# Light convolution and maxout on one core: tokens loaded with the rows ahead of them, weights split in twelve units, and a new opening order

## The chip, the cores and the metric

One core of a Trainium2 chip runs the whole program. Its engines are named as the profile names them: PE (TensorE, with PEld for its weight loads), DVE (VectorE), ACT (ScalarE), POOL (GpSimd) and SP (SyncE, which here issues nearly all DMAs and passes signals between matmuls). The metric is the device time of one execution in microseconds (us), lower is better; given is the median of several runs.

## The reference

`x` is 8 x 4160 tokens of 192 numbers, `weight_gen` has 8 heads x 7 taps for each token. The first half is a causal light convolution with softmaxed taps, the second a maxout layer. Cut to what matters:

```python
w = weight_gen - np.max(weight_gen, axis=-1, keepdims=True)
w = np.exp(w)
w = w / (np.sum(w, axis=-1, keepdims=True) + 1e-09)
x_pad = np.concatenate([np.zeros((B, 6, D), np.float32), x], axis=1)
idx = np.arange(S)[:, None] + np.arange(7)[None, :]
x_unf = x_pad[:, idx, :].reshape(B, S, 7, H, group)
x = np.einsum('bshk,bskhg->bshg', w, x_unf).reshape(B * S, D)
h = np.maximum(np.maximum(x @ w1, x @ w2), x @ w3)
return (h @ w_out).astype(np.float32)
```

`w1`, `w2`, `w3` (192 x 768) and `w_out` (768 x 192) arrive as 64-bit floats: each value is two 32-bit words, the high one with sign, exponent and the first mantissa bits.

## The kernel before, in words

**Tiling.** The 33,280 tokens lie on 128 partitions, 260 consecutive tokens each; 16 partitions hold one batch. Work goes in 65 chunks of 4 tokens per partition (512 tokens). Loads go in groups of chunks ("supers"): chunk 0 alone, then three chunks each. A group's tile `xt` holds its tokens and the 6 ahead of them, `wt` its taps.

**Attention half of a chunk.** `softmax(s)` (L210) works on a whole group: a maximum on DVE (`red`), a subtraction on POOL, Exp on ACT, sum, addition and reciprocal on DVE (`den`), a product on POOL. `product(c, t)` (L234, "x") multiplies the taps of one token on POOL into `r`; `total(c, t)` (L257, "+") sums `r` over the taps on DVE into `acc`. `transpose(c)` ("t") brings `acc` to features on partitions, for chunks 0 to 2 with PE into two banks of PSUM, later with DVE and ACT. `parts(c)` (L293, "p") makes a high and a low part of it (`xa_hi`, `xa_lo`, `xb`, `xc`), which for chunks 0 to 2 costs ACT four copies and DVE two subtractions.

**Maxout half.** `up` (L341) makes 18 outputs of 128 features x 512 tokens in PSUM (`ph`, 8 buffers that everything in PSUM shares), each from 9 matmuls on half the rows of the array; two chains of half-row matmuls run side by side. Of the three outputs of one block, ACT copies the first to `m` (L376) and DVE takes the maximum with the second and the third (L378), so a chunk has 12 such maxima. Then ACT and POOL make `h_hi` and `h_lo` (L381, L385), and `down` (L389) multiplies them by `w_out`; the products of chunk c - 1 stand after the twelfth output of chunk c.

**Weights.** Before the matmuls of chunk 0 can go on, each weight must be split into a high and a low fp32r part. `split` (L453) does it for 18 units: `a0` to `a8` (rows 0 to 127 of w1 to w3, 256 columns each), `b0` to `b2` (rows 128 to 191, 384 columns), `d0` to `d5` (`w_out`, 192 columns). Each unit costs ACT an Abs (L470), a copy of half-words (L476), the high part (L493) and a conversion (L497), DVE five operations (L481, L483, L488, L494, L495) and POOL a product (L498); a `b` unit also needs four copies on ACT to both halves of the partitions (L553).

**The order.** All instructions are pinned in the order in which the program writes them. Time is counted in ticks, 22 to a chunk; `OPENING` names for the first ticks what is written at each (one step of a unit, product, sum and so on), with -1 for all that stands ahead of the first matmul. After the opening fixed ticks place everything. Each engine takes its own instructions strictly in this order.

**Loads.** `load_super` (L183) fills `xt` of a group. Where the group begins within the first 6 tokens of a partition, the rows ahead lie at the end of the partition before: DVE sets them to zero (L196), one DMA of 128 partitions brings the tokens (L197), and 8 DMAs, one for each batch and 15 partitions each, bring the rows ahead (L202). For group 0, half of these 8 stand on ACT's queue. The raw words of the weights go into buffers that are used later for other things (`h_hi`, `h_lo`, `raw_a`, `room`).

Of the kernel before, what the change touches and what calls it, by code (L numbers as in the profile page):

```python
# [21 lines left out]
P = 128  # L22

OPENING = {
    -1: (
# [1 line left out]
        "a1 b0 s0 b1 +0.2 s1 a3 a3 a6"  # L30
# [79 lines left out]

# [20 lines left out]

# [573 lines left out]
```

## Time and profile before

| | |
|---|---|
| median of 3 runs | 1697.91 us (1697.88 to 1699.43) |
| the profiled execution, its own time | 1699.39 us |
| its span, first to last instruction | 1697.6 us |
| PE busy in the span | 1657.2 us (98%) |
| DVE, ACT, POOL busy | 1124.6, 1145.8, 1426.2 us |
| first matmul of chunk 0 | 29.96 us |
| first matmul of `down` for chunk 0 | 81.86 us |

The profile gives one execution. A row of its groups says how often an instruction ran, its mean in ns and how long the engine stood idle before it; a row of its timeline begins with the start and the duration in us; a row by windows gives busy us and the number of instructions of each engine in a stretch. Matmuls are pipelined, so two hundred of them in 20 us and a hundred in 20 us can both look busy: in the opening the count is what to read.

### The profile page before, as it was taken

The numbers are of one execution on the slowest core, as the hardware profiler recorded it, in microseconds if no ns is written. First come the engines' busy times: TensorE is split into PE (matmuls) and PEld (weight loads), VectorE is DVE, ScalarE is ACT, GpSimd is POOL, SyncE is SP. The second block draws the span as 40 slices with busy tenths as digits, with TensorE's granted clock in tenths as the row PEclk, the third lists the DMA queues.
The fourth block names the chain that finished last, engine by engine and source line by source line (L and its number), as shares of the span: only waits on it lengthen the run. The fifth ranks groups of instructions, "written<-read, shape, count | busy, mean of one in ns | idle before, by whom it ended". The sixth has DMA issues, their size and how long they took to land.

```text
span 1697.6 us, 42191 instructions
## 1 busy us (share of the span) xinstructions
PE 1657.2 (98%) x16794; PEld 1466.1 (86%) x16794; DVE 1124.6 (66%) x1552; ACT 1145.8 (67%) x2896; POOL 1426.2 (84%) x844
## 2 busy tenths in 40 slices
PE   3899999999999999999999999999999999999999
PEld 2598889889889889889988988988988988988998
DVE  7966766666666666666666666666666666666653
ACT  5657667667666766766766766766776776676672
POOL 6888888989888888888888888988888888888872
PEclk9999999999999999999999999999999999999999
DMA  7010101101010110101010110101011010101000
GB/s 236 1 70 10 70 29 52 70 20 60 20 70 15 66 70 21 60 21 70 11 70 21 60 70 20 61 20 70 11 70 61 27 63 20 70 11 46 20 11 29
DMA packets 20422, 79.51 MB, mean 47 GB/s; under 512 B 2320, under 2 KB 5128, under 8 KB 17536
## 3 DMA queue, kind: packets, MB, share of 16 engines
q1 hardware_dynamic: 20104, 76.54, 11.9%
q8 instruction: 131, 2.15, 0.5%
q14 instruction: 67, 0.55, 0.1%
q10 hardware_dynamic: 120, 0.28, 0.0%
HBM read 51.25 MB, written 25.56 MB: 45 GB/s over the span
## 4 chain that ended last, share of the span: by engine, by line
PE 94%; DVE 3%; ACT 1%; DMA 1%; POOL 1%; SPq 0%; issue 0%; DVEq 0%
PE ph L329 94%; DVE acc L261 1%; DVE m L378 0%; DMA wt<-in_weight_gen_dram 0%; DVE ph L483 0%; POOL r L246 0%; DVE ph L488 0%; DVE e L495 0%; DVE ph L481 0%; DVE ph L494 0%; DMA xt<-in_x_dram 0%; SPq L529 0%; ACT room L290 0%; SPq L521 0%; POOL h_lo L385 0%
## 5 line engine op out<-in xcount | busy, mean ns | idle before, releaser
L246 POOL TENSOR_TENSOR r<-xt,wt 128x1344 f32<-128x1344 f32 x260 | 721.4, 2814 | 0.6 <-DMA xt<-in_x_dram 0.4
L378 DVE TENSOR_TENSOR m<-ph,m 128x512 f32<-128x512 f32 x780 | 520.6, 685 | 197.4 <-PE ph L329 113.7
L329 PE MATMUL ph<-xa_hi,wa_hi 64*128 64x512 f32 x2340 | 630.8, 391 | 9.4 <-DVE m L378 3.1
L385 POOL TENSOR_TENSOR h_lo<-m,h_hi 128x512 fp32r<-128x512 f32 x390 | 503.3, 1301 | 161.7 <-ACT h_hi L381 157.0
L329 PE MATMUL ph<-xa_lo,wa_hi 64*128 64x512 f32 x2340 | 626.9, 388 | 1.0 <-DVE xa_lo L304 1.0
L329 PE MATMUL ph<-xa_hi,wa_lo 64*128 64x512 f32 x2340 | 626.1, 387 | 1.1 <-POOL wa_lo L498 1.1
L329 PE MATMUL ph<-xb,wb_hi 64*128 64x512 f32 x2340 | 626.0, 387 | 0.0
L329 PE MATMUL ph<-wo,h_hi 64*128 64x384 f32 x3120 | 595.5, 355 | 0.0
L329 PE MATMUL ph<-wo,h_lo 64*128 64x192 f32 x3120 | 522.3, 247 | 0.0
L381 ACT CAST h_hi<-m 128x512 fp32r<-128x512 f32 x390 | 241.8, 621 | 409.7 <-DVE m L378 406.6
L261 DVE TENSOR_REDUCE acc<-r 128x192 f32<-128x1344 f32 x260 | 401.8, 1547 | 125.5 <-POOL r L246 125.5
L290 ACT COPY room<-room 32x128 f32<-32x128 f32 x1488 | 440.8, 296 | 25.7 <-DVE room L284 7.5
L329 PE MATMUL ph<-xc,wb_lo 64*128 64x512 f32 x1170 | 453.1, 387 | 0.1
L329 PEld LDWEIGHTS ph<-wo,h_lo 64*128 64x128 f32 x3120 | 398.8, 188 | 2.5
L329 PEld LDWEIGHTS ph<-wo,h_hi 64*128 64x128 f32 x3120 | 398.4, 184 | 2.9 <-issue 0.4
L329 PEld LDWEIGHTS ph<-xa_hi,wa_hi 64*128 64x128 f32 x2340 | 338.7, 185 | 53.9 <-DVE m L378 3.9
L329 PEld LDWEIGHTS ph<-xa_hi,wa_lo 64*128 64x128 f32 x2340 | 338.4, 185 | 42.0 <-POOL wa_lo L498 1.5
L329 PEld LDWEIGHTS ph<-xa_lo,wa_hi 64*128 64x128 f32 x2340 | 338.7, 185 | 38.7 <-DVE xa_lo L304 1.5
L329 PEld LDWEIGHTS ph<-xb,wb_hi 64*128 64x128 f32 x2340 | 338.7, 185 | 38.4 <-ACT xb L308 0.3
L376 ACT COPY m<-ph 128x512 f32<-128x512 f32 x390 | 221.8, 586 | 38.5 <-PE ph L329 35.3
L411 DVE TENSOR_TENSOR o<-ph,ob 128x192 f32<-128x192 f32 x260 | 86.7, 353 | 234.5 <-ACT ob L410 234.5
L329 PEld LDWEIGHTS ph<-xc,wb_lo 64*128 64x128 f32 x1170 | 216.3, 185 | 20.9 <-POOL wb_lo L498 0.5
(54 smaller groups left out, 702.6 us busy)
## 6 DMA issues: line engine op xcount, KB each, us to landing
xt<-in_x_dram SPq DMA_DIRECT2D x20, 1728.0 KB, 7.1
out_dram<-o SPq DMA_DIRECT2D x64, 384.0 KB, 2.3
wt<-in_weight_gen_dram SPq DMA_DIRECT2D x21, 336.0 KB, 3.0
h_hi<-in_moe_w_dram SPq DMA_DIRECT2D x6, 256.0 KB, 4.8
xt<-in_x_dram SPq DMA_DIRECT2D x1, 1536.0 KB, 9.3
h_lo<-in_moe_w_dram SPq DMA_DIRECT2D x6, 192.0 KB, 4.8
room<-in_moe_w_out_dram SPq DMA_DIRECT2D x1, 1152.0 KB, 8.1
xt<-in_x_dram SPq DMA_DIRECT2D x1, 960.0 KB, 5.2
```

Of the source, the lines that this page charges most:

```text
L246: nc.gpsimd.tensor_tensor(r.rearrange("p (h g) k -> p k h g", g=G), xt[:, la + t : la + t + K].rearrange("p k (h g) -> p k h g", g=G), wt[ ...
L261: nc.vector.tensor_reduce(state["acc", c][:, t], r, axis=AX.X, op=ALU.add)
L290: pin(nc.scalar.copy(to[:, :, p : p + 32], blocks[p : p + 32, :, f : f + 32]))
L329: ins = nc.tensor.matmul(ph[:, :n], w[h], v[h], start=begins and half == 0 and q == 0, stop=ends and half == 1 and q == len(terms) - 1,)
L376: pin(nc.scalar.copy(m[:, :N], ph[:, :N]))
L378: pin(nc.vector.tensor_tensor(m[:, :N], ph[:, :N], m[:, :N], op=ALU.max))
L381: later(1, lambda: pin(nc.scalar.copy(hi, m[:, :N])))
L385: nc.gpsimd.tensor_tensor(lo, m[:, :N], hi.bitcast(F32), op=ALU.subtract)
L411: pin(nc.vector.tensor_tensor(o[:, t], po[:, :D], ob, op=ALU.add))
```

## The change

**Loads of groups 0 and 1.** A partition's tokens and the 6 (or 2) rows ahead of them are contiguous in memory, so each partition now loads both with one run: one DMA for partitions 16 to 127 (112), one for 1 to 15, one for partition 0, all on SP. What comes from the batch before is then cleared: for group 0 by `clear` ("c0"), two operations on DVE that mask with `inside` (0 on the first partition of a batch); for group 1 by a DMA of zeros taken from `ident`. `inside` comes from an iota on POOL and two small operations on DVE. ACT's table for Exp is loaded by an early activation on one column.

**Groups.** Chunk 1 is a group of its own, so chunks 2 to 4 are the next. The sum of the softmax of the first three groups lies in PSUM.

**Split.** 12 units: `a0` to `a5` (256 or 512 columns), `b0` to `b2` and `d0` to `d2` (384 each). In the six units of `WHOLE`, Abs takes its scale 2^-112 and DVE clamps once (`min`); in the other six the clamp is two Relu on ACT. Then follow on DVE two `scalar_tensor_tensor`, on ACT the high part (`d2` on DVE) and the low part as a difference, on POOL for `a4`, `b0`, `b2`, `d0` and on DVE for the others. The high part of a `b` unit is used from where it lies for one half; the other half comes by two DMAs (`b0`, `b1`) or two copies on ACT (`b2`) instead of four.

**Order.** The loads stand as `s0 a0 b s1 a1 a2 d` (before: `s0 a0 b a1 s1 a2 d`), and `OPENING` is new. The diff, cut to its core:

```diff
 OPENING = {
     -1: (
-        "x0.0 x0.1 a0 a0 a1 a0 a1 x0.3 a2 a0 x0.2 a2 +0.0 a2 b0 b0 s1 +0.1 a1 a2 b0 +0.3 s1 "
+        "x0.3 a0 x0.0 a0 a1 a0 a0 a0 b2 a1 +0.3 a1 a0 a1 x0.2 t0 s1 b2 x0.1 a1 a1 b2 b1 b1 "
...
+LO_ON_POOL = ("a4", "b0", "b2", "d0")
+BY_DMA = ("b0", "b1")
+HI_ON_VECTOR = ("d2",)
+WHOLE = ("a0", "a1", "a2", "a4", "b1", "b2")
+FIRST = 2
+LOADS = "s0 a0 b s1 a1 a2 d"
+UNITS_A = ((0, 0, 1), (0, 1, 3), (1, 0, 2), (1, 2, 3), (2, 0, 2), (2, 2, 3))
+UNITS_D = ((0, 2), (2, 4), (4, 6))
...
-        if len(supers) == 1 or len(supers[-1]) == SC:
+        if len(supers) <= FIRST or len(supers[-1]) == SC:
...
-            pin(nc.vector.memset(xt[:, :z], 0.0))
-            pin(nc.sync.dma_start(out=xt[:, z : n + PAD], in_=xf[:, : a + n]))
-            for b in range(B):
-                queue = nc.scalar if s == 0 and b % 2 else nc.sync
...
+            for p, q in ((PB, P), (1, PB)):
+                pin(nc.sync.dma_start(out=xt[p:q, : n + PAD], in_=rows[p - 1 : q - 1]))
+            pin(nc.sync.dma_start(out=xt[:1, z : n + PAD], in_=xf[:1, : a + n]))
+            if s == 0:
+                pin(nc.vector.memset(xt[:1, :z], 0.0))
...
+    def clear(s):
+        n = PAD // 2
+        for t in (n, 0):
+            xs = state["x", s][:, t : t + n].rearrange("p t d -> p (t d)").bitcast(I32)
+            pin(nc.vector.tensor_tensor(
+                    xs, xs, inside.broadcast_to([P, n * D]), op=ALU.bitwise_and))
+            yield
+    def clear_by_dma(s, n):
...
+        pin(nc.sync.dma_start(out=xt, in_=zeros))
...
+    def split(flat, hi, lo, name, into, **sizes):
...
+            scale = 2.0**-112 if whole else 1.0
+            pin(nc.scalar.activation(u, high.bitcast(F32), AF.Abs, scale=scale))
+        if whole:
+            pin(nc.scalar.activation(low, halfwords[..., 1], AF.Copy, scale=7.49 / 65536))
+        else:
...
+            pin(eng(to, halfwords[..., 1:3]))
+        yield
...
+        if whole:
+            pin(eng.tensor_scalar(u, u, W_MAX, None, op0=ALU.min))
+            parts = (u.bitcast(U32), 3, low, ALU.logical_shift_left)
+        else:
...
+                pin(nc.scalar.activation(u, upper, AF.Relu, bias=over, scale=-1.0))
+                yield
+                upper, bias, scale = u, span, -float(1 << 19)
+            pin(nc.scalar.activation(v.bitcast(U32), upper, AF.Relu, bias=bias, scale=scale))
+            parts = (low, 13, v.bitcast(U32), ALU.logical_shift_right)
+        yield
+        pin(nc.vector.scalar_tensor_tensor(
+                v.bitcast(U32), *parts[:3], op0=parts[3], op1=ALU.bitwise_or))
+        yield
+        w = prep.tile([P, NU], F32, name="w", bufs=3)[:, :n] if name in LO_ON_POOL else v
+        pin(nc.vector.scalar_tensor_tensor(
...
+        w = w.rearrange(into, **sizes)
+        if name in HI_ON_VECTOR:
+            pin(nc.vector.tensor_copy(hi, w))
+        else:
+            pin(nc.scalar.copy(hi, w))
+        yield
+        eng = nc.gpsimd if name in LO_ON_POOL else nc.vector
+        pin(eng.tensor_tensor(lo, w, hi.bitcast(F32), op=ALU.subtract))
```

What this moves shows in three places. On DVE, the opening up to the first sum of a token; this was the order before (L481 to L495 are the split of `a0` and `a1`, `f` and `e` its intermediate values, L261 the sum of products `r`):

```order
L481 TENSOR_SCALAR ph<-ph 128x256
L483 TENSOR_SCALAR ph<-ph 128x256
L488 SCALAR_TENSOR_TENSOR ph<-h_hi,ph 128x256
L494 TENSOR_SCALAR ph<-f 128x256
L495 TENSOR_SCALAR e<-ph 128x256
```

And this is the order now (L182 clears the rows ahead in `xt`, L468, L484, L491 and L508 are a split, L246 is the sum):

```order
L182 TENSOR_TENSOR xt<-xt,edges 128x576 x2
L468 TENSOR_SCALAR ph<-ph 128x256
L484 SCALAR_TENSOR_TENSOR ph<-ph,low 128x256
L491 SCALAR_TENSOR_TENSOR ph<-h_hi,ph 128x256
L468 TENSOR_SCALAR ph<-ph 128x512
L246 TENSOR_REDUCE acc<-r 128x192
L484 SCALAR_TENSOR_TENSOR ph<-ph,low 128x512
L508 TENSOR_TENSOR wa_lo<-ph,wa_hi 128x2x128
```

The five operations of a unit on DVE became two to four, three in most units, and for eight of the twelve units one of them is the low part, which stood on POOL.

On DVE again, around the 14th to 16th maximum of the program (L378, `m_718` and `m_702`; chunk 0 has twelve, so these are of chunk 1), before. The other rows are splits of `w_out`, each `ph` number a unit, `f` and `e` their intermediate values:

```order
L378 TENSOR_TENSOR m_718<-ph_705,m_718 128x512
L481 TENSOR_SCALAR ph_751<-ph_751 128x192
L483 TENSOR_SCALAR ph_751<-ph_751 128x192
L488 SCALAR_TENSOR_TENSOR ph_751<-room_88,ph_751 128x192
L378 TENSOR_TENSOR m_702<-ph_716,m_702 128x512
L481 TENSOR_SCALAR ph_755<-ph_755 128x192
L483 TENSOR_SCALAR ph_755<-ph_755 128x192
L488 SCALAR_TENSOR_TENSOR ph_755<-room_88,ph_755 128x192
L378 TENSOR_TENSOR m_718<-ph_739,m_718 128x512
L494 TENSOR_SCALAR ph_751<-f_753 128x192
L495 TENSOR_SCALAR e_752<-ph_751 128x192
```

The same place now, from the last split to the 16th maximum (L359 is the maximum, `m_630` and `m_646` those of the 13th to 16th; L484 to L508 is the end of the split of `d2`, L288 and L293 the parts of chunk 2, L246 a sum of chunk 3):

```order
L484 SCALAR_TENSOR_TENSOR ph_303<-low_304,ph_303 128x384
L491 SCALAR_TENSOR_TENSOR ph_303<-room_89,ph_303 128x384
L503 CAST wo_84<-ph_303 128x2x192
L508 TENSOR_TENSOR wo_84<-ph_303,wo_84 128x2x192
L288 TENSOR_TENSOR xa_lo_667<-ph_656,xa_hi_666 128x512
L293 TENSOR_TENSOR xb_668<-ph_657,xc_669 64x512
L359 TENSOR_TENSOR m_630<-ph_614,m_630 128x512
L359 TENSOR_TENSOR m_646<-ph_633,m_646 128x512
L246 TENSOR_REDUCE acc_706<-r_704 128x192
L359 TENSOR_TENSOR m_630<-ph_644,m_630 128x512
L359 TENSOR_TENSOR m_646<-ph_684,m_646 128x512
```

All splits now stand ahead of the 13th maximum, and the parts of chunk 2 with them; before, nine operations of splits stood behind the 16th.

On SP, the queue of loads before (L189 are taps, L197 tokens, L202 the rows ahead, L521 and L529 weights):

```order
L189 DMA wt<-in_weight_gen_dram 128x224
L197 DMA xt<-in_x_dram 128x768
L202 DMA xt<-in_x_dram 15x1152 x4
L521 DMA h_hi<-in_moe_w_dram 128x512 x3
L529 DMA h_lo<-in_moe_w_dram 64x3x256 x6
L521 DMA h_hi<-in_moe_w_dram 128x512 x3
L189 DMA wt<-in_weight_gen_dram 128x672
L197 DMA xt<-in_x_dram 128x3072
L202 DMA xt<-in_x_dram 15x384 x8
```

And now (L160 are taps, L170 and L171 tokens with the rows ahead, L532 and L540 weights):

```order
L160 DMA wt<-in_weight_gen_dram 128x224
L170 DMA xt<-in_x_dram 112x1920
L170 DMA xt<-in_x_dram 15x1920
L171 DMA xt<-in_x_dram 1x768
L532 DMA h_hi<-in_moe_w_dram 128x512 x3
L540 DMA h_lo<-in_moe_w_dram 64x3x256 x6
L160 DMA wt<-in_weight_gen_dram 128x224
L170 DMA xt<-in_x_dram 112x1920
L170 DMA xt<-in_x_dram 15x1920
L171 DMA xt<-in_x_dram 1x1536
L532 DMA h_hi<-in_moe_w_dram 128x512 x3
L532 DMA raw_a<-in_moe_w_dram 128x512 x3
```

Six DMAs of SP and four of ACT ahead of the first weights became four of SP. Behind the rows shown stand `w_out`, the zeros for group 1, the taps and tokens of group 2 (chunks 2 to 4), and only then the four DMAs that bring the other halves of `b0` and `b1`.

More of the change, by code (lines that the diff above doesn't have):

```diff
@@ L169, in lightconv_maxout_kernel @@
     wo = const.tile([P, NJ, 2 * D], F32R, name="wo")
-    F_MAX = float(np.array(0x47EFFFFF, np.uint32).view(np.float32))
-    F_MIN = float(np.array(0x38000000, np.uint32).view(np.float32))
-    NU = 3 * P
+    E_MIN = (1023 - 127) << 4
+    E_MAX = (255 << 4) - 1
+    NU = 4 * P
+    edges = const.tile([P, P], F32, name="edges")
+    over, span, below, warm = (edges[:, k : k + 1] for k in range(4))
+    inside = edges[:, 4:5].bitcast(I32)
+    F_MAX = float(np.array((E_MIN + E_MAX) << 16 | 0xFFFF, np.uint32).view(np.float32))
+    W_MAX = float(np.array(255 << 20, np.uint32).view(np.float32) * (1 - 2.0**-24))
     halves = (slice(0, DB), slice(DB, P))
@@ L259, in total @@
         r = state.pop(("r", c, t))
+        if ("acc", c) not in state:
+            state["acc", c] = att.tile([P, TC, D], F32, name="acc")
         pin(
@@ L348, in up @@
             j = 2 * jp + odd
-            terms = [(wa_hi[:, j, i], xa_hi), (wa_hi[:, j, i], xa_lo), (wb_hi[:, j, i], xb)]
+            terms = [(wa_hi[:, j, i], xa_hi), (wa_hi[:, j, i], xa_lo)]
+            terms.append((wb_hi[:, j if half == 0 else j ^ 1, i], xb))
             if half == odd:
@@ L540, in prepare_a @@
     def prepare_a(u):
-        jp, i = divmod(u, 3)
-        raw = raws_a[jp][:, i].rearrange("p (j n) w -> p j n w", j=2)
-        pair = slice(2 * jp, 2 * jp + 2)
-        yield from split(raw, wa_hi[:, pair, i], wa_lo[:, pair, i])
-    def prepare_b(jp):
-        raw = raw_b[:, jp]
-        hi = prep.tile([P, 3, P], F32R, name="hi", bufs=1)
-        yield from split(raw, hi, wb_lo[:, jp])
-        for odd, h in enumerate(halves):
-            for to in halves:
-                pin(nc.scalar.copy(wb_hi[to, 2 * jp + odd], hi[h].bitcast(F32)))
@@ new lines, in prepare_b @@
+    def prepare_b(jp):
+        flat = raw_b[:, jp].rearrange("p i n w -> p (i n) w")
+        hi, other = (wb_hi[:, 2 * jp + odd] for odd in range(2))
+        yield from split(flat, hi, wb_lo[:, jp], f"b{jp}", "p (i n) -> p i n", n=P)
+        yield
+        for h, to in zip(halves, reversed(halves)):
+            if f"b{jp}" in BY_DMA:
+                pin(nc.sync.dma_start(out=other[to].bitcast(F32), in_=hi[h].bitcast(F32)))
+            else:
+                pin(nc.scalar.copy(other[to], hi[h].bitcast(F32)))
@@ L566, in lightconv_maxout_kernel @@
+    nc.gpsimd.memset(span, float(E_MAX << 19))
+    nc.gpsimd.memset(below, float(-(E_MIN << 19)))
+    pin(nc.scalar.activation(warm, below, AF.Exp))
+    state["now"] = -1
+    for name in LOADS.split():
+        if name[0] == "s":
+            load_super(int(name[1:]))
+        elif name[0] == "a":
+            load_up(int(name[1:]))
+        else:
+            {"b": load_rest, "d": load_down}[name]()
     make_identity(nc, ident)
+    clear_by_dma(1, PAD - TC)
     NC = len(chunks)
@@ L585, in stage @@
             finish(f"s{super_of[c]}")
+            if c == 0 and t[0] == PAD // 2:
+                if "c0" not in running:
+                    stage("c0")
+            elif c == 0:
+                finish("c0")
         elif name[0] == "+":
```

182 lines of the change are left out of this document (74 added, 108 removed), and 23 rows, old and new, of the table OPENING.

## The prediction, as put on record

> **What bounds the kernel now.** First the windows of the trace, core 0: busy us and number of instructions of PE, PEld, DVE, ACT and POOL, then the granted clock, the DMA share and GB/s.
>
> ```profile
> 30.00:40.00 10.00, 8.84 (x41) 6.28 (x43) 9.55 (x20) 7.38 (x17) 8.57 (x5) 1.00 0.62 243
> 50.00:60.00 10.00, 7.39 (x54) 4.46 (x52) 9.65 (x20) 8.07 (x18) 4.22 (x5) 1.00 0.00 1
> 70.00:80.00 10.00, 8.03 (x58) 5.68 (x56) 9.35 (x23) 5.93 (x17) 10.00 (x9) 0.88 0.00 0
> 80.00:90.00 10.00, 10.00 (x111) 8.73 (x109) 5.91 (x9) 3.94 (x8) 8.24 (x6) 0.95 0.01 2
> 400.00:800.00 400.00, 400.00 (x4106) 356.33 (x4103) 264.15 (x354) 277.82 (x708) 347.74 (x202) 1.00 0.13 49
> ```
>
> In the steady part PE runs 10.26 matmuls per us. Between 30 and 80 us it runs 41 to 58 in 10 us, though it counts as busy there, and DVE is at 93 to 97%. From 80 us on PE is at full rate and DVE at 59%. So the kernel has an opening that DVE bounds and a long part that PE bounds. Next the waits of PE from 100 to 1600 us (us in total, times, longest), then the end of the chain of waits, and from PE's timeline the first matmul of `down`:
>
> ```profile
> PE ph L329 <- DVE o L411: 0.2, 1, 0.2
> ```
> ```profile
> 170.18 1523.98 PE ph L329 x14710
> ```
> ```profile
> 81.86 0.44 PE L329 MATMUL ph<-wo,h_hi 64*128 64x384 f32 x1
> ```
>
> PE waits 0.2 us in 1500, and the chain stays on PE to the end. So the time is that of the first `down` plus a constant, as long as the other engines keep ahead of PE behind it: what the first `down` gains, the kernel gains. I cost the change as the move of 81.86, in three stretches.
>
> **The start of DVE's splits.** The timeline of SP's queue, ACT, DVE and POOL (start, duration, what ended the idle time):
>
> ```profile
> 2.09 3.59 SPq L202 DMA_DIRECT2D xt<-in_x_dram  x4
> ...
> 6.08 1.51 SPq L521 DMA_DIRECT2D h_hi<-in_moe_w_dram  x3
> ```
> ```profile
> 4.02 1.28 ACT L222 ACT_TABLE_LOAD   x1 [4.02 <-DVE red L215]
> ...
> 8.70 0.40 ACT L470 ACTIVATE ph<-h_hi 128x256 f32<-128x256 f32 x1 [3.00 <-DMA h_hi<-in_moe_w_dram]
> ```
> ```profile
> 9.14 0.43 DVE L481 TENSOR_SCALAR ph<-ph 128x256 f32<-128x256 f32 x1 [2.42 <-ACT ph L470]
> ```
> ```profile
> 7.84 7.65 POOL L246 TENSOR_TENSOR r<-xt,wt 128x1344 f32<-128x1344 f32 x3 [0.40 <-DMA xt<-in_x_dram]
> ```
>
> The first weights left SP at 6.08, behind four issues of rows ahead, 3.59 us together. Now four single issues stand there; at 0.4 to 0.9 us each the weights leave at about 3, and would land at 5.7 by the same 2.6 us of flight. Against that, the tokens are two and a half times the bytes, and DVE has two clears (128x576) ahead of the first split, which wait for the tokens. I take them at 0.7 us each, by the nearest row (128x512, 0.68, below), and the tokens at 6.5 us. POOL's first product shows them complete at 7.84 before. Then DVE starts to split at 8.3, with 7.2 (tokens 1.1 us earlier than that) and 10.5 (2.2 later) as bounds. Gain 0.8, from -1.4 to 1.9. The table load, 1.28 us on ACT behind the first `red`, now stands at the start, where ACT waits anyway; it hides behind the DMAs and is worth nothing, unless the tokens come first.
>
> **DVE from there to the 16th maximum.** The groups of DVE up to 90 us (count, busy us, mean ns, idle before), and the 16th maximum in its timeline:
>
> ```profile
> L261 DVE TENSOR_REDUCE acc<-r 128x192 f32<-128x1344 f32 x12 | 18.3, 1543 | 0.0
> L378 DVE TENSOR_TENSOR m<-ph,m 128x512 f32<-128x512 f32 x20 | 13.3, 683 | 1.7 <-PE ph L329 1.6
> ...
> L488 DVE SCALAR_TENSOR_TENSOR ph<-h_hi,ph 128x256 uint32<-128x256 uint32 x6 | 2.6, 429 | 0.2
> ...
> L488 DVE SCALAR_TENSOR_TENSOR ph<-room,ph 128x192 uint32<-128x192 uint32 x6 | 2.2, 362 | 0.2
> ...
> L304 DVE TENSOR_TENSOR xa_lo<-ph,xa_hi 128x512 fp32r<-128x512 f32 x3 | 2.0, 681 | 0.0
> ...
> L215 DVE TENSOR_REDUCE red<-wt 128x96 f32<-128x672 f32 x2 | 1.7, 850 | 0.1
> L488 DVE SCALAR_TENSOR_TENSOR ph<-h_lo,ph 128x384 uint32<-128x384 uint32 x3 | 1.7, 562 | 0.1
> L481 DVE TENSOR_SCALAR ph<-ph 128x384 f32<-128x384 f32 x3 | 1.7, 559 | 0.5 <-ACT ph L470 0.5
> ...
> L226 DVE RECIPROCAL den<-den 128x96 f32<-128x96 f32 x1 | 0.8, 752 | 0.0
> ```
> ```profile
> 74.29 0.68 DVE L378 TENSOR_TENSOR m<-ph,m 128x512 f32<-128x512 f32 x1
> ```
>
> A split operation takes 0.43, 0.36 or 0.56 us at 256, 192 or 384 columns; those of one width agree within 0.02. Before, 90 of them: 45 x 0.43 + 30 x 0.36 + 15 x 0.56 = 38.6, of which nine of 0.36 (3.2) stand behind the 16th maximum. So from 9.14 on: splits 35.3, ten sums 15.4, softmax of group 1 and the `red` of group 2 3.5, parts of two chunks 2.7, 16 maxima 10.9, together 67.8, in 65.8 us (74.97 - 9.14; neighbours overlap a little): a ratio of 0.97.
>
> Now, with 0.69 for 512 columns (by L378): `a1`, `a2` four operations and `a4` three, 7.6; `a0` four, `a3`, `a5` three, of 0.43, 4.3; the `b` and `d` units 18 of 0.56, 10.1: 39 operations, 22.0. With them 13 sums (20.0), the softmax of group 1, now a third as wide (1.3), and of group 2 (2.7), parts of three chunks (4.1) and 16 maxima (10.9): 61.0, times 0.97 is 59.2. So three more sums, a pair of parts and part of a softmax, pulled ahead, take back 7.6 of the 13.3 us that the splits give. Gain 6.6. If the new kinds (a 32-bit mask with a shift and an or, a subtraction into half a tile) take a fifth longer than their width says, 4.4 less; if as the narrower of their neighbours, 2 more.
>
> Six clamps go to ACT, two Relu each. ACT's rows for the same width are no slower:
>
> ```profile
> L470 ACT ACTIVATE ph<-h_lo 128x384 f32<-128x384 f32 x3 | 1.6, 524 | 1.8 <-DMA h_lo<-in_moe_w_dram 1.8
> ...
> L553 ACT CAST wb_hi<-hi 64x384 fp32r<-64x384 f32 x12 | 6.1, 508 | 0.2
> ```
>
> Twelve Relu at 0.4 to 0.52 are some 6 us on an engine that is 59 to 81% busy in the windows above, and that loses ten of the L553 copies (5.1) and the conversions (L497); DVE saves 2 x 0.43 + 4 x 0.56 = 3.1. I cost it at nothing. The Trainium skill, "ScalarE: Activation LUTs", section Rules for kernel authors, has relu and min belong on VectorE instead of ScalarE. By that rule these 3.1 us would not be gained and the total gain would be about 11 instead of 14; the rows above differ by 0.035 us at this width, so the trace has no price for the move, and I keep the 3.1.
>
> **From the 16th maximum to the first `down`.** Before, 74.97 to 81.86, 6.9 us. PE's timeline in it:
>
> ```profile
> 77.67 0.80 PE L329 MATMUL ph<-xa_hi,wa_hi 64*128 64x512 f32 x2 [0.99 <-ACT m L376]
> ...
> 79.54 1.04 PE L329 MATMUL ph<-xa_hi,wa_hi 64*128 64x512 f32 x2
> ```
>
> Nine operations of `w_out`'s splits stood behind the maximum, a copy of ACT waited for one of them, and PE went on at 77.67. It then ran 16 matmuls in the 3.5 us up to 81.2, which at 10.26 per us take 1.6: 1.9 us lost at the lower granted clock (0.88 in the window). Now no split stands there. The outputs ahead of the first `down` need buffers that the parts of chunk 2 and the 13th and 14th maximum free, and the first `down` needs the one that the 15th frees, so with eight buffers PE runs six outputs ahead and `down` can begin about when the 16th maximum runs. I take 0.2 us, gain 6.7; at worst the six outputs (9 matmuls, 0.88 us each) all stand behind it and the gain is 1.6. The Trainium skill, "TensorE: Matmul & The Clock Gate", section on the HAM clock gate, says that the clock falls to half after an idle window of about 3.4 us. By that rule one such pause would cost the 1.9 us again and two 3.9; the trace agrees with the halving (0.42 us between pairs at 79 us), and which pauses remain no row here shows.
>
> Sum: 0.8 + 6.6 + 6.7 = 14.1, so the first `down` at 67.7.
>
> **What has to stay hidden.** POOL's groups up to 90 us:
>
> ```profile
> L246 POOL TENSOR_TENSOR r<-xt,wt 128x1344 f32<-128x1344 f32 x14 | 37.7, 2727 | 0.5 <-DMA xt<-in_x_dram 0.4
> L385 POOL TENSOR_TENSOR h_lo<-m,h_hi 128x512 fp32r<-128x512 f32 x10 | 12.8, 1283 | 1.8 <-ACT h_hi L381 1.8
> L498 POOL TENSOR_TENSOR wa_lo<-f,e 128x256 fp32r<-128x256 f32 x9 | 6.5, 724 | 7.1 <-ACT f L497 7.1
> ...
> L217 POOL TENSOR_TENSOR wt<-wt,red 128x672 f32<-128x672 f32 x2 | 2.7, 1364 | 2.7 <-DVE red L215 2.7
> L229 POOL TENSOR_TENSOR wt<-wt,den 128x672 f32<-128x672 f32 x1 | 1.4, 1356 | 3.5 <-DVE den L226 3.5
> ```
>
> Up to the last `h_lo` of chunk 0, POOL has twelve products (32.8), two softmax (3.9), four low parts (4.3 by the 0.72 and 1.0 us of L498) and six `h_lo` (7.7): 48.7 us, from 8 to 57 without a wait, against 67.7. Its idle times before come to some 20 us over a longer stretch, so the slack of 11 covers them only in part; I expect 4 to 8 of idle time, since fourteen of the eighteen products of splits that it waited for are gone.
>
> The loads: the copies that bring the halves of `b0` and `b1` stand behind the load of group 2, and DVE's `red` of group 2 waits for those taps with everything behind it. Before, the loads ended about here:
>
> ```profile
> 36.00:39.00 3.00, 2.88 (x21) 2.04 (x20) 2.91 (x7) 2.32 (x6) 3.00 (x2) 1.00 0.09 37
> ```
>
> DVE reaches that `red` at about 29. With SP's eight issues of rows ahead of group 1 gone, and tokens of five chunks in the first three groups instead of seven, I put the taps at 27 to 28 and the copies at 33, needed by 38.
>
> **The rivals.** *PE does not run ahead* (0.17): the 16th maximum comes as I say, but the copies of ACT or the transposes hold PE back and the 6.9 us stay: a gain of 7.4, 1690.5. For it: in the windows PE has never been ahead of DVE. *The loads are late* (0.10): if the taps of group 2 land with the last load as before, at 36, DVE stands 7 us: a gain of 7, 1691. For it, a clump of bigger loads; against, SP's shorter queue. *The stretch is not DVE's* (0.07): rounds through ACT, DVE and PE set the pace, and the fewer operations leave gaps (the idle column of L378, 1.7, is the only sign): 1696 to 1698. *Slower, POOL becomes the bound* (0.05): products stand in front of `h_lo` in its order; if its idle time passes 28 us instead of 20 (57 + 28 = 85), the first `down` comes at 85 or later, and the time is 1702. The forecast itself has 0.61.
>
> **How the numbers follow.** The profiled execution took 1699.39 us, its span 1697.6; the median is 1697.91, 1.5 lower. The sum gives 1685.3 against the profiled one and 1683.8, in round numbers 1684, against the median. The three terms' bounds give 1680 to 1688 for the forecast alone; the first two rivals reach to 1691, so 1680 to 1692 leaves out the last two and a little below. About 0.2% (3.4 us) is what a measurement of this kernel can tell from no change. Faster by more than that: 0.61 + 0.17 + 0.10 = 0.88; the same 0.07; slower 0.05.
>
> **What would show it.** First split on DVE near 8.3, 16th maximum near 67.5, first `down` within 1 us of it, then at once 100 matmuls and more in 10 us. Wrong, if DVE's idle time in the opening grows over some 4 us, if the split operations exceed 24 us, or if PE waits again behind 100 us, where the first `down` would no longer set the end.

## The result, and the profile after

The changed kernel takes 1685.40 us (median of 4 runs, 1685.15 to 1685.79) against 1697.97 us before (4 runs, 1697.88 to 1699.43): the ratio is 0.9924, its 95% interval 0.9907 to 0.9941, so it is faster by 12.6 us. The forecast was 1684.0 with a range of 1680 to 1692. The profiled execution took 1685.41 us, its span 1683.6, 14.0 less than before. That is 1.4 more than the medians differ by, since the profiled execution of before took 1699.39 us and its median is 1697.97; in which stretch this 1.4 us lies, no second trace shows.

The windows of core 0 in the opening of the changed kernel, in the same columns as in the prediction:

```profile
30.00:40.00 10.00, 6.42 (x22) 4.86 (x24) 9.90 (x17) 9.13 (x18) 10.00 (x7) 1.00 0.23 67
40.00:50.00 10.00, 10.00 (x86) 8.02 (x84) 9.45 (x12) 6.73 (x13) 9.92 (x6) 1.00 0.56 213
50.00:60.00 10.00, 10.00 (x91) 8.23 (x88) 9.76 (x13) 4.27 (x9) 8.48 (x6) 1.00 0.00 0
60.00:70.00 10.00, 10.00 (x89) 8.05 (x87) 9.43 (x14) 5.07 (x10) 10.00 (x6) 1.00 0.01 2
70.00:80.00 10.00, 10.00 (x126) 10.00 (x124) 8.09 (x13) 4.94 (x16) 9.92 (x6) 1.00 0.01 2
```

PE runs 86 to 91 matmuls in 10 us from 40 us on, where it ran 54 to 70 before (the prediction's "41 to 58" leaves out two of the five windows, 40 to 50 with 60 and 60 to 70 with 70), and it has no gap any more. That is its full rate: a pair of matmuls starts every 0.23 us, as in the steady part, and in this stretch there is no `down`, whose smaller matmuls raise the count of the steady part to 102. DVE is as busy as it was. PE's timeline at the start of that run and at the first `down`, and two rows of the chain of waits:

```profile
36.51 0.80 PE L309 MATMUL ph<-xa_hi,wa_hi 64*128 64x512 f32 x2 [1.91 <-DVE w L491]
...
69.63 0.33 PE L309 MATMUL ph<-wo,h_hi 64*128 64x384 f32 x1
```
```profile
36.51 8.94 PE ph L309 x62
...
62.32 1617.56 PE ph L309 x15710
```

From 36.51 on PE waits for nothing, and the chain is PE's alone to the end (between the two rows stand only its matmuls and transposes). So in this trace the first `down` comes 33.1 us behind the start of PE's run, all of it PE's own time, and what the start waited for is a split on DVE (L491). Not all of that time is at full rate. PE's timeline shows when:

```profile
38.81 1.02 PE L309 MATMUL ph<-xa_lo,wa_hi 64*128 64x512 f32 x2
39.24 0.94 PE L309 MATMUL ph<-xb,wb_hi 64*128 64x512 f32 x2
...
40.25 0.41 PE L309 MATMUL ph<-xa_hi,wa_hi 64*128 64x512 f32 x2
40.48 0.41 PE L309 MATMUL ph<-xa_lo,wa_hi 64*128 64x512 f32 x2
```

Until 40.0 a pair starts every 0.43 us, behind it every 0.23: PE ran at half speed for the first 3.5 us, though the window's granted clock says 1.00. The first `down` came 12.2 us earlier, not 14.1; the rest of the 14.0 lies behind it. Before, 1615.7 us passed from the first `down` to the end of the span (1697.6 - 81.86); now 1614.0 (1683.6 - 69.63). In the trace of before the first matmuls of `down` of successive chunks come 26.0, 25.4, 25.6 and 25.7 us behind each other and then every 25.2 us; in the changed kernel they come every 25.2 us from the first one on. So the 1.8 us are lost in the first four chunks behind the first `down`.

DVE's timeline at its first split and its 15th and 16th maximum:

```profile
8.34 1.43 DVE L182 TENSOR_TENSOR xt<-xt,edges 128x576 int32<-128x576 int32 x2 [2.95 <-DMA xt<-in_x_dram]
9.69 0.43 DVE L468 TENSOR_SCALAR ph<-ph 128x256 f32<-128x256 f32 x1
...
67.33 1.28 DVE L359 TENSOR_TENSOR m<-ph,m 128x512 f32<-128x512 f32 x2
```

The 16th maximum ends at 68.6, 58.9 us behind the first split, and the first `down` follows 1.0 us later. The first split itself came at 9.69, later than the 9.14 of before.

### The profile page after: what moved, and what is told of

Read it like the earlier page. It is cut to its first block, busy times and chain, and to the rows that moved or that the text cites. A ratio compares the mean times of both kernels' runs of the same rounds, so it can differ in the third digit from the quotient of the medians.

```text
span 1683.6 us, 42090 instructions
## 1 busy us (share of the span) xinstructions
PE 1651.1 (98%) x16794; PEld 1640.7 (97%) x16794; DVE 1109.6 (66%) x1504; ACT 1136.8 (68%) x2862; POOL 1418.9 (84%) x834
## 4 chain that ended last, share of the span: by engine, by line
PE 98%; DMA 1%; DVE 0%; ACT 0%; issue 0%; SPq 0%
PE ph L309 97%; DMA h_hi<-in_moe_w_dram 0%; DMA xt<-in_x_dram 0%; DMA h_lo<-in_moe_w_dram 0%; DVE ph L484 0%; DVE ph L491 0%; ACT ph L457 0%; ACT low L459 0%; PE ph L260 0%; ACT low L463 0%; ACT xc L290 0%; PE ph L261 0%; DVE red L200 0%; DVE acc L246 0%; DVE ph L468 0%
## 5 line engine op out<-in xcount | busy, mean ns | idle before, releaser
L359 DVE TENSOR_TENSOR m<-ph,m 128x512 f32<-128x512 f32 x780 | 520.5, 685 | 204.3 <-PE ph L309 118.5
L309 PE MATMUL ph<-xa_hi,wa_hi 64*128 64x512 f32 x2340 | 623.3, 389 | 3.0 <-DVE w L491 1.9
L309 PE MATMUL ph<-wo,h_lo 64*128 64x192 f32 x3120 | 551.8, 247 | 0.0
L246 DVE TENSOR_REDUCE acc<-r 128x192 f32<-128x1344 f32 x260 | 401.7, 1547 | 124.6 <-POOL r L229 124.6
L309 PEld LDWEIGHTS ph<-wo,h_lo 64*128 64x128 f32 x3120 | 458.6, 188 | 0.0
L309 PEld LDWEIGHTS ph<-wo,h_hi 64*128 64x128 f32 x3120 | 453.7, 184 | 0.0
L309 PEld LDWEIGHTS ph<-xa_hi,wa_hi 64*128 64x128 f32 x2340 | 358.0, 184 | 5.7 <-ACT ph L457 2.6
L309 PEld LDWEIGHTS ph<-xa_lo,wa_hi 64*128 64x128 f32 x2340 | 357.4, 185 | 2.1 <-DVE xa_lo L288 1.1
L309 PEld LDWEIGHTS ph<-xb,wb_hi 64*128 64x128 f32 x2340 | 357.3, 184 | 2.0 <-ACT wb_hi L505 0.8
L309 PEld LDWEIGHTS ph<-xa_hi,wa_lo 64*128 64x128 f32 x2340 | 357.3, 184 | 1.5 <-issue 0.4
```

The costliest lines, as they stand in the source:

```text
L246: nc.vector.tensor_reduce(state["acc", c][:, t], r, axis=AX.X, op=ALU.add)
L309: ins = nc.tensor.matmul(ph[:, :n], w[h], v[h], start=begins and half == 0 and q == 0, stop=ends and half == 1 and q == len(terms) - 1,)
L359: pin(nc.vector.tensor_tensor(m[:, :N], ph[:, :N], m[:, :N], op=ALU.max))
```

## The experiments

Theory D is the prediction's: DVE takes its instructions in order, and its work up to the 16th maximum sets the first `down`. The first rival, theory P, came from the trace above: PE waits for nothing from 36.5 us on, so only what delays that start counts, and DVE has slack behind it. Others (L, W, B) are named where they are tested. All runs change the changed kernel; times are medians, to be set against 1685.40.

| run | time, us | start of PE's run | at half speed from there | PE's waits behind the start | first `down` | from there to the end of the span |
|---|---|---|---|---|---|---|
| changed kernel | 1685.40 | 36.51 | 3.5 | 0 | 69.63 | 1614.0 |
| sum_later | 1686.92 | 35.63 | 4.4 | 0.9 | 70.89 | 1614.2 |
| d0_later | 1688.40 | 35.88 | 3.6, up to its wait | 2.05 | 71.56 | 1614.0 |
| dve_early | 1687.79 | 38.43 | 4.8 | 0 | 72.13 | 1613.9 |
| dve_late1 | 1686.59 | 39.19 | 5.7 | 0.5 | 74.11 | 1613.9 |
| dve_late | 1690.11 | 36.30 | 5.2 | 2.6 | 74.91 | 1614.0 |
| clamp_dve | 1687.23 | 37.59 | 5.6 | 0 | 71.81 | 1613.7 |
| clear_dve | 1686.27 | 36.31 | 6.1 | 0 | 70.68 | 1613.9 |
| old_loads | 1688.42 | 38.79 | 6.1 | 0 | 73.09 | 1613.7 |
| act_copies | 1686.61 | 37.99 | 4.3 | 0 | 71.46 | 1613.7 |
| d_pool | 1687.62 | 36.67 | 5.7 | 0 | 70.81 | 1617.6 |
| a_d_pool | 1688.96 | 37.80 | 4.4 | 0 | 71.36 | 1616.0 |
| pool_late | 1692.88 | 36.36 | 4.4 | 0 | 69.91 | 1620.9 |

The columns behind the time are of the one profiled execution of each. That of dve_late1 took 1689.80 us and its loads landed late, so its start and its 74.11 say nothing of the edit; that of d_pool took 1690.14.

Half speed is the time until a pair of PE's matmuls starts every 0.23 us instead of every 0.43, read from PE's timeline of each run. By these two numbers a microsecond of it costs 0.47 us (an estimate). Where PE has no wait behind its start, the start and this cost together give the first `down` within about 0.1 us: in old_loads the start is 2.3 us later and the half speed 2.6 us longer (1.2 us), 3.5 together, and the first `down` is 3.5 later. The half speed lasts 3.5 to 6.1 us, and the changed kernel's trace has the shortest. Whether an edit lengthens it or it differs between executions of one kernel, one trace of each can't tell.

So a difference of about 1 us isn't by itself the price of an edit. There is a second reason: the changed kernel was not measured again beside these runs. The kernel before was, and its medians were 1698.08 to 1698.67, 0.1 to 0.7 above the 1697.97 of the result.

**A sum moved behind the start of PE's run (sum_later).**

```diff
-    1: "a3 p0 a4 b1 a5 a5 a4 s2 b1 +1.1 a5 d0 d0 a1 b1 d0",
+    1: "a3 p0 a4 b1 a5 a5 a4 s2 b1 a5 d0 d0 a1 b1 d0",
-    2: "s2 s1 d0 a4 s0 b1 a3 d2 a3 a5 a2 a5 d1 d0 a5 a4 s2 +1.0 x1.3 d1 d0 b2 +1.2",
+    2: "s2 s1 d0 a4 s0 b1 a3 d2 a3 a5 a2 a5 d1 d0 a5 a4 s2 +1.0 +1.1 x1.3 d1 d0 b2 +1.2",
```

> The changed kernel with the second sum of chunk 1 (token 1) moved in DVE's order from ahead of the last splits that the first matmuls need to behind the softmax of group 2: DVE has the same work up to the 16th maximum, but 1.5 us less of it ahead of 36.4 us. Theory P (PE runs without a pause from 36.5 us on, so the end is set by when PE can start, and DVE's total up to the 16th maximum is not the bound): the start moves to about 35.1, the first `down` from 69.6 to about 68.3, the time from 1685.4 to about 1684.1. Theory D (the prediction's: DVE's total up to the 16th maximum sets the first `down`): no change, 1685.4.

Measured: 1686.92, 1.5 slower, as neither theory had it. POOL's timeline, then PE's:

```profile
39.17 2.83 POOL L229 TENSOR_TENSOR r<-xt,wt 128x1344 f32<-128x1344 f32 x1 [3.93 <-DVE acc L246]
41.84 1.27 POOL L508 TENSOR_TENSOR wa_lo<-w,wa_hi 128x512 fp32r<-128x512 f32 x1
```
```profile
35.63 0.79 PE L309 MATMUL ph<-xa_hi,wa_hi 64*128 64x512 f32 x2 [1.39 <-ACT ph L457]
...
42.94 0.49 PE L309 MATMUL ph<-xa_hi,wa_hi 64*128 64x512 f32 x1 [0.66 <-SPq L320]
```

PE did start 0.9 us earlier. But it ran 0.9 us longer at half speed, and the sum that was moved frees one of the three buffers of `r`: POOL's next product stood 3.9 us for it, and behind the product stands the low part of `a4`, which came at 41.84 instead of 37.96; PE paused until 42.94, about when it was done (the ends of POOL's rows are rough).

**The split of d0 moved instead (d0_later).** In the diff, the seven steps of `d0` go behind the softmax of group 2:

```diff
-    1: "a3 p0 a4 b1 a5 a5 a4 s2 b1 +1.1 a5 d0 d0 a1 b1 d0",
+    1: "a3 p0 a4 b1 a5 a5 a4 s2 b1 +1.1 a5 a1 b1",
-    2: "s2 s1 d0 a4 s0 b1 a3 d2 a3 a5 a2 a5 d1 d0 a5 a4 s2 +1.0 x1.3 d1 d0 b2 +1.2",
+    2: "s2 s1 a4 s0 b1 a3 d2 a3 a5 a2 a5 d1 a5 a4 s2 +1.0 x1.3 d1 d0 d0 b2 +1.2 d0 d0 d0 d0",
```

> The changed kernel with the split of the first third of w_out (d0) moved behind the start of PE's long run, on ACT (four operations), DVE (two, 1.1 us) and in its buffer of PSUM; DVE's work up to the 16th maximum is the same, and no product or sum moves, so POOL keeps its buffers in time. In the run with a sum moved, POOL stood 3.9 us for one of its three buffers and the start of PE, though 0.9 us earlier, brought nothing: this move is free of that. Theory P (the start of PE's run sets the end): the start moves from 36.5 to about 35.2 and the time from 1685.4 to about 1684.2. Theory D (DVE's total up to the 16th maximum sets it): no change, 1685.4.

Measured: 1688.40 (1686.51 to 1689.86 in five runs), slower again. PE's timeline:

```profile
35.88 0.80 PE L309 MATMUL ph<-xa_hi,wa_hi 64*128 64x512 f32 x2 [1.36 <-DVE wa_lo L508]
...
42.13 0.49 PE L309 MATMUL ph<-xa_hi,wa_hi 64*128 64x512 f32 x2 [2.05 <-DVE w L491]
```

The split holds a buffer of PSUM until its L491. Moved, it held the buffer that PE's next output wanted, and PE stood 2.05 us at 42. So an earlier start brought nothing in either run; but both brought a wait of their own, so neither shows what a start without one would give, and neither settles theory P.

**More work on DVE, early and late (dve_early, dve_late, dve_late1).** The loop is put around each sum, with another list for each run; shown is dve_early, dve_late has (2, 1), (2, 2), (2, 3), dve_late1 only (2, 1):

```diff
+        for _ in range(2 if (c, t) in ((0, 0), (0, 3)) else 1):
             pin(
                 nc.vector.tensor_reduce(
                     state["acc", c][:, t], r, axis=AX.X, op=ALU.add
```

> The changed kernel with the first two sums done twice (same result), 3.0 us more work on DVE between 12 and 20 us. Theory P and theory D both: 3.0 us later, 1688.4, if DVE's queue is what sets PE's start at 36.5. Theory L (the landing of the weights, to which the chain of waits leads back between 8 and 22 us, sets it): DVE makes up for part of it in waits for loads, under 1.5 us, below 1686.9.

> The changed kernel with three sums of chunk 2 done twice (same result), 4.5 us more work on DVE between 49 and 57 us. Theory D: the 16th maximum and the first `down` come 4.4 us later, 1689.8. Theory P: PE only notices once DVE's delay exceeds what its eight buffers cover; DVE is 97% busy from 50 to 60 us, so some of it should show, 0 to 2 us, 1685.4 to 1687.4.

> The changed kernel with one sum of chunk 2 done twice (same result), 1.5 us more work on DVE at 49 us. With three sums more (4.4 us) the first `down` came 5.3 us later: PE waited 2.6 us for maxima and ran at a granted clock of 0.5 to 0.7 for 4 us behind a pause. Theory D: DVE has no slack, 1.5 us later, 1686.9. Theory P: the buffers of PSUM cover about the first 1.5 us, so under 0.4 us, 1685.4 to 1685.8.

Measured: 2.4 us more for 3.0 early, 4.7 for 4.4 late, 1.2 for the 1.5 of a single sum late. Theory D had 3.0, 4.4 and 1.5; theory P had 3.0, up to 2.0 and under 0.4; theory L had under 1.5 for the early one. By the times theory D is nearest. The traces don't bear its sizes out: PE's run began 1.9 us later in dve_early, and in dve_late PE waited 2.6 us for maxima, not 4.4. In dve_late, PE's timeline and the windows around its longest wait:

```profile
53.25 0.50 PE L310 MATMUL ph<-xa_hi,wa_hi 64*128 64x512 f32 x2 [0.52 <-DVE m L360]
...
61.74 0.71 PE L310 MATMUL ph<-xa_hi,wa_hi 64*128 64x512 f32 x2 [2.07 <-DVE m L360]
```
```profile
58.00:60.00 2.00, 1.66 (x16) 1.04 (x12) 1.97 (x3) 0.00 (x0) 0.00 (x0) 1.00 0.00 0
60.00:62.00 2.00, 0.26 (x2) 0.27 (x4) 2.00 (x3) 0.00 (x0) 0.00 (x0) 0.96 0.00 0
62.00:64.00 2.00, 2.00 (x12) 1.54 (x12) 2.00 (x5) 0.62 (x2) 0.00 (x0) 0.50 0.00 0
64.00:66.00 2.00, 2.00 (x16) 1.59 (x14) 1.97 (x3) 1.30 (x3) 1.93 (x2) 0.68 0.00 0
```

The first extra sum (1.5 us, at 49.5) made PE wait 0.5 us at 53.25, and the trace of dve_late1 has the same wait of 0.5 us: about 1 us of a late sum is covered there. Behind the long pause the granted clock stood at 0.50 and 0.68 in the two windows; a pair started every 0.43 us from 61.74 to 65.23, some 1.6 us lost, and the start of the run was at half speed 1.7 us longer. So PE's waits for DVE explain 2.6 of the 5.3 us by which the first `down` came later, and the slower clock most of the rest. Theory P had too little for both (up to 2.0 and under 0.4, against waits of 2.6 and 0.5), so it falls as it was put; but that theory D had nearly the right times is in part luck.

**The clamps back on DVE (clamp_dve).**

```diff
-CLAMP_ON_VECTOR = ()
+CLAMP_ON_VECTOR = ("a3", "a5", "b0", "d0", "d1", "d2")
```

> The changed kernel with the clamp of the six units on DVE (one min each, 2 x 0.43 + 4 x 0.56 = 3.1 us) instead of the first of two Relu on ACT; four of the six (2.0 us) stand ahead of the start of PE's run. The prediction costed the move to ACT as a gain of 3.1 us at no price: by it and theory D the time grows by 3.1 us to 1688.5. Theory P: by about 2.0 us, 1687.4. The rule of the Trainium skill that such operations belong on VectorE: no slower, 1685.4 or less.

Measured: 1687.23, 1.8 slower, nearest to theory P's 2.0; the first `down` is at 71.81. DVE got 3.1 us more and ACT lost six Relu. In the trace PE's run begins 1.1 us later and is at half speed 2.1 us longer. So moving the clamps to ACT is worth at most 1.8 us by the medians, not the 3.1 of the sum, and it is no loss.

**The rows ahead of group 1 cleared on DVE (clear_dve).**

```diff
-        n = PAD // 2
-        for t in (n, 0):
+        n = PAD // 2 if s == 0 else PAD - TC
+        for t in (n, 0) if s == 0 else (0,):
...
-    clear_by_dma(1, PAD - TC)
```

> The changed kernel with the rows ahead of group 1 cleared by one operation on DVE (128x384, 0.55 us, near 20 us) instead of a DMA of zeros, for which POOL stood 3.6 us at 24 us. Theory D and theory P: DVE has 0.55 us more and may wait for the tokens of group 1 up to 0.7 us, POOL's pause was covered: 0.5 to 1.2 us slower, 1685.9 to 1686.6. Theory W (POOL's products are what the opening waits for): POOL is 3 us earlier and the time falls by 1 to 2 us, 1683.4 to 1684.4.

Measured: 1686.27, 0.9 slower, the size that theories D and P had, but the trace doesn't show their cause. PE's run begins 0.2 us earlier; its timeline has the half speed until 42.4, 2.6 us longer than in the changed kernel:

```profile
40.71 0.66 PE L309 MATMUL ph<-xa_lo,wa_hi 64*128 64x512 f32 x2
41.14 0.66 PE L309 MATMUL ph<-xb,wb_hi 64*128 64x512 f32 x2
...
42.70 0.61 PE L309 MATMUL ph<-xb,wb_hi 64*128 64x512 f32 x2
42.93 0.39 PE L309 MATMUL ph<-xc,wb_lo 64*128 64x512 f32 x1
```

So what the clear costs isn't shown. In the changed kernel POOL's timeline has

```profile
27.14 2.65 POOL L229 TENSOR_TENSOR r<-xt,wt 128x1344 f32<-128x1344 f32 x1 [3.58 <-DMA xt<-ident]
```

and without that wait this product came 3.5 us earlier and the start of PE's run 0.2: the pause is covered, and theory W falls for this place. The clear took 0.76 us on DVE. (The run also sets the rows of the first partition to zero on POOL; the diff leaves that line out.)

**The old loads of groups 0 and 1 (old_loads).** The new lines of `load_super` and both clears give way to the removed ones. The run also pins the loads of the weights in the order in which they are written, which neither kernel does:

```diff
-            for p, q in ((PB, P), (1, PB)):
-                pin(nc.sync.dma_start(out=xt[p:q, : n + PAD], in_=rows[p - 1 : q - 1]))
...
+            pin(nc.vector.memset(xt[:, :z], 0.0))
+            pin(nc.sync.dma_start(out=xt[:, z : n + PAD], in_=xf[:, : a + n]))
+            for b in range(B):
...
```

> The changed kernel with the tokens of groups 0 and 1 loaded as before (zeros by DVE, 128 partitions, 8 DMAs of rows ahead for each group, half of the first 8 on ACT's queue), no clears, and the other loads in the order of before the change's text. The prediction's step: the first split starts 0.8 us later than in the changed kernel. By the traces as they are (first split at 9.69 with the new loads and at 9.14 with the old ones) it starts about 0.5 us earlier. Theory D: about 0.5 us faster or, if the second half of the weights comes late, slower. Theory L: SP issues the rows ahead of group 1 in some 9 us ahead of the weights a1, which land near 27 instead of 22 us, and the time grows by 3 to 5 us, 1688 to 1690.

Measured: 1688.42, 3.0 slower, as theory L had it. SP's timeline, then DVE's and PE's:

```profile
12.61 6.20 SPq L173 DMA_DIRECT2D xt<-in_x_dram  x8
18.85 1.34 SPq L528 DMA_DIRECT2D h_hi<-in_moe_w_dram  x3
```
```profile
9.32 0.43 DVE L464 TENSOR_SCALAR ph<-ph 128x256 f32<-128x256 f32 x1 [3.35 <-ACT ph L453]
...
29.27 0.43 DVE L480 SCALAR_TENSOR_TENSOR ph<-low,ph 128x256 uint32<-128x256 uint32 x1 [1.96 <-ACT ph L476]
```
```profile
38.79 0.80 PE L305 MATMUL ph<-xa_hi,wa_hi 64*128 64x512 f32 x2 [2.26 <-DVE w L487]
```

DVE's first split came 0.4 us earlier, and it did not help. The eight DMAs of group 1 kept SP 6.2 us, the weights `a1` left it at 18.85 instead of 13.06, and at 29 DVE stood 2 us for a Relu on ACT, behind them. PE's run began 2.3 us later and was at half speed 2.6 us longer. So the new loads are worth up to 3.0 us, 2.3 of it by the queue behind group 1 and none by the start of the splits.

**Copies on ACT instead of DMAs (act_copies).**

```diff
-BY_DMA = ("b0", "b1")
+BY_DMA = ()
```

> The changed kernel with the other halves of b0 and b1 copied by ACT (four copies of 0.51 us) instead of four DMAs. The prediction took the DMAs as hidden, needed by 38 us, and costed ACT's savings at nothing: then the time stays within 0.5 us, 1685.0 to 1685.9. If ACT is short in the opening (it was 91% busy from 30 to 40 us): 1 to 2 us slower, 1686.4 to 1687.4.

Measured: 1686.61, 1.2 slower. DVE's timeline, then PE's:

```profile
34.93 0.56 DVE L484 SCALAR_TENSOR_TENSOR ph<-low,ph 128x384 uint32<-128x384 uint32 x1 [1.22 <-ACT ph L480]
```
```profile
37.99 0.80 PE L309 MATMUL ph<-xa_hi,wa_hi 64*128 64x512 f32 x2 [3.38 <-DVE w L491]
```

Four copies (2.0 us) on ACT make DVE wait 1.2 us for a Relu, and PE's run begins 1.5 us later. So ACT is short around 30 us.

**DVE relieved by POOL and ACT (d_pool, a_d_pool).** The second run has "a1" in the list as well:

```diff
-LO_ON_POOL = ("a4", "b0", "b2", "d0")
+LO_ON_POOL = ("a4", "b0", "b2", "d0", "d1", "d2")
-HI_ON_VECTOR = ("d2",)
+HI_ON_VECTOR = ()
```

> The changed kernel with the low parts of d1 and d2 on POOL and the high part of d2 on ACT: three operations of 0.56 us less on DVE between 57 and 63 us, 2.1 us more on POOL ahead of the last `h_lo` of chunk 0, and one copy more on ACT. Theory D (DVE's work up to the 16th maximum sets the first `down`): 0.9 to 1.7 us faster, 1683.7 to 1684.5. Theory P, or if POOL's two operations hold up `h_lo`: no gain, 1685.4 to 1686.4.

> As the run with d1 and d2, and the low part of a1 on POOL as well (0.68 us less on DVE at 17 us, 1.3 more on POOL, ahead of POOL's pause at 24 us). Theory D: 0.5 us faster than that run and 1.4 to 2.3 us faster than the changed kernel, 1683.1 to 1684.0. If what matters is only what stands ahead of the start of PE's long run: 0.5 us faster than the changed kernel, 1684.9.

Measured: 1687.62 (1686.64 to 1690.14) and 1688.96 (1686.67 to 1689.50), at least 1.2 slower in every run. Theory D had a gain. POOL's timeline of the changed kernel and of d_pool, then DVE's and PE's of d_pool:

```profile
61.45 10.85 POOL L229 TENSOR_TENSOR r<-xt,wt 128x1344 f32<-128x1344 f32 x4
```

```profile
64.50 1.02 POOL L508 TENSOR_TENSOR wo<-w,wo 128x384 fp32r<-128x384 f32 x1 [2.09 <-ACT wo L505]
65.47 10.80 POOL L229 TENSOR_TENSOR r<-xt,wt 128x1344 f32<-128x1344 f32 x4
```
```profile
64.04 0.69 DVE L288 TENSOR_TENSOR xa_lo<-ph,xa_hi 128x512 fp32r<-128x512 f32 x1 [1.24 <-ACT xa_hi L284]
...
68.30 1.55 DVE L246 TENSOR_REDUCE acc<-r 128x192 f32<-128x1344 f32 x1 [0.76 <-POOL r L229]
```
```profile
79.50 0.50 PE L309 MATMUL ph<-xa_hi,wa_hi 64*128 64x512 f32 x1 [1.73 <-DVE m L359]
```

What DVE no longer does, it waits for: first for ACT, then for products of POOL, which begin 4 us later (65.5 instead of 61.5) because POOL stands for a copy of ACT. Behind the first `down` PE stands 1.7 us in both traces; in d_pool the granted clock is then 0.50 from 80 to 82 us and 0.66 from 82 to 84, in a_d_pool it stays at 1.00, and the span behind the first `down` is 1617.6 against 1616.0. The later first `down` of d_pool (1.2 us) is that of a longer half speed (5.7 against 3.5 us), not of these waits.

**POOL late behind the first `down` (pool_late).**

```diff
+        for _ in range(2 if c == 4 else 1):
             pin(
                 nc.gpsimd.tensor_tensor(
```

> The changed kernel with the four products of chunk 4 done twice (same result): 11 us more work on POOL behind the first `down`. The kernel before took 1615.7 us from its first `down` to the end of the span; the changed kernel and all eight runs so far took 1613.7 to 1614.2. At 8 us behind the first `down` the kernel before had done 14 products, the changed one 18. Theory B (the kernel before lost 1.8 us behind its first `down` because POOL was four products late): the first `down` stays at 69.6 and the span behind it grows by 1 to 3 us, time 1686.4 to 1688.4. If POOL's lateness is covered (what the prediction took for granted): 1685.4.

Measured: 1692.88, 7.5 slower; the first `down` stayed (69.91) and the span behind it grew from 1614.0 to 1620.9. The waits of PE up to 1600 us and the windows around the longest:

```profile
PE ph L310 <- DVE m L360: 4.3, 1, 4.3
```
```profile
94.00:96.00 2.00, 0.00 (x0) 0.00 (x0) 0.65 (x1) 0.86 (x2) 2.00 (x2) 0.86 0.00 0
96.00:98.00 2.00, 0.44 (x2) 0.45 (x4) 2.00 (x3) 0.00 (x0) 2.00 (x3) 0.50 0.00 0
98.00:100.00 2.00, 2.00 (x12) 1.51 (x12) 1.30 (x3) 1.27 (x3) 2.00 (x1) 0.50 0.00 0
100.00:102.00 2.00, 2.00 (x14) 1.61 (x12) 0.69 (x1) 0.92 (x2) 1.92 (x2) 0.50 0.00 0
```

So lateness of POOL there does reach the end: DVE waits for a product, a maximum comes behind its sum, PE for the maximum. The size was 6.9 us of 11, not 1 to 3: 4.3 us of waiting and some 2 us by the granted clock of 0.50, at which a pair started every 0.43 us from 97.6 to 101.6 (an estimate). That the kernel before lost its 1.8 us this way fits: 8 us behind the first `down` its POOL had done 14 products (to 90 us, in the prediction's groups), the changed one (to 77.77 us) 17, one fewer than the expectation counted:

```profile
L229 POOL TENSOR_TENSOR r<-xt,wt 128x1344 f32<-128x1344 f32 x17 | 46.2, 2780 | 6.9 <-DMA xt<-ident 3.6 <-DVE xt L182 3.1
```

and its chain of waits leaves PE once more behind the opening, through POOL:

```profile
152.77 0.69 DVE m L378
...
155.48 5.48 POOL r L246 x2
```

The kernel before itself was not tried with less work on POOL, and there is one trace of it, so for its 1.8 us the cause is argued, not shown.

## Why the prediction was right, and where its steps were not

*Where the time is.* Right: the opening, and the first `down` plus a constant. In nine of the twelve experiments the constant was 1613.7 to 1614.2, whatever happened ahead of it. It was no constant between the two traces: 1.8 us of the 14.0 came from behind the first `down`. The prediction took it for granted that the other engines keep ahead of PE there; the kernel before did not quite, and pool_late, d_pool and a_d_pool show what it costs when they don't.

*The start of the splits*, 0.8 us gained: wrong, 0.55 lost (9.69 against 9.14). The weights left SP at 2.42, as forecast, but landed no earlier:

```profile
2.42 1.30 SPq L532 DMA_DIRECT2D h_hi<-in_moe_w_dram  x3
```
```profile
8.67 0.40 ACT L457 ACTIVATE ph<-h_hi 128x256 f32<-128x256 f32 x1 [4.33 <-DMA h_hi<-in_moe_w_dram]
```

The flight of 2.6 us was taken from weights that left SP 3.7 us later. The tokens were not the difference: the two and a half times of the prediction counts one DMA of before and leaves out the eight with the rows ahead, and with them the bytes are 0.95 MB before and 0.98 now. But the weights now stand behind tokens still in flight (from 2 to 8 us the DMA engines were 99 to 101% busy, 58 to 86% before), and their flight was 6.2 us. And DVE takes the two clears, which waited for the tokens until 8.34 (taken as 6.5), ahead of the split. What the loads did give, up to 3.0 us by old_loads, lay elsewhere: the prediction named SP's shorter queue only as cover for the taps of group 2.

*DVE to the 16th maximum*, 59.2 us: the size is right, 58.9, and so is its main part, 39 split operations with 21.6 us against 22.0. That this length sets the first `down` is only half of what the runs show. In the changed kernel PE waits for no maximum: DVE sets the start of PE's run, and from there PE's own 33.1 us reach the first `down`. DVE stays so close ahead that late work on it does reach PE, less about 1 us for one sum (dve_late). Three things in the step don't hold. Relieving DVE gave nothing further: d_pool and a_d_pool made DVE wait for ACT and POOL instead, and sum_later and d0_later ended in waits for a buffer of `r` and one of PSUM. The yardstick of 102 matmuls in 10 us for PE was too high for a stretch without `down`: its full rate is 86 to 91. And no term of the sum holds PE's half speed at the start of its run, 3.5 us, some 1.6 us lost. Two slips of the text did not enter the sum or the forecast: the work pulled ahead takes back 6.5 us by its own terms, not 7.6, and ACT's busy share reaches 89% in the window from 40 to 50 us, which isn't among those that gave 59 to 81%.

*Edits costed at nothing.* The clamps: by clamp_dve the move gains 1.8 of 3.1 us at most; whether the other 1.3 is the price on ACT, no run separates. The Trainium skill, "ScalarE: Activation LUTs", section Rules for kernel authors, sends such operations to VectorE. Here the measurement speaks against it: DVE is over 93% busy in the opening and sets the start of PE's run, which came 1.1 us later with the clamps back on VectorE (up to 1.8 us by the medians). The copies by DMA were hidden as forecast, but that they come off ACT was worth about 1.2 us, not nothing. The zeros for group 1 by DMA cost POOL 3.6 us that were covered.

*From the 16th maximum to the first `down`*, 0.2 us: 1.0, a gain of 5.9 instead of 6.7. The mechanism held: no split stands behind it, and PE runs without a pause.

*The sum.* +0.55, -6.9 and -5.9 make -12.2 where -14.1 was forecast; the missing 1.9 and the 1.8 behind the first `down` cancel, by luck. The traces then differ by 14.0, the medians by 12.6, and the forecast of 1684 is 1.4 too low. The range has a slip of its own: all three terms at their worst leave a gain of 2.4 us (-1.4, 2.2 and 1.6), or 1695.5, so its 1688 is not what the bounds give.

*The rivals.* "PE does not run ahead" did not happen. "The loads are late" did not happen, though old_loads shows its mechanism, with `a1` in place of the taps. "POOL becomes the bound" did not happen in the changed kernel (POOL's idle time ahead of the last `h_lo` of chunk 0 was some 5 us behind its first product, 4 to 8 were forecast), but a moved sum is enough for a wait of 3.9 us.

What stays open: no run puts back the old splits or the old order, so that they bring the larger part of the gain is read from the two traces and from the count of DVE's operations, not shown by taking them away; the runs price the loads, the clamps and the copies alone. Why the half speed lasts 3.5 us in one trace and 6.1 in another is open too. So is whether an order exists in which PE's run begins earlier without a new wait; four edits that relieve DVE or the way to that start (sum_later, d0_later, d_pool, a_d_pool) were all slower.
